# One low part queued earlier and seven w_sp units summed later in an fp32 FNet + gMLP kernel

## The chip, the cores and the metric

The kernel runs on one core of one Trainium2 chip. Its time is the device time of one execution in microseconds (us). Before the change it took 959.19 us, the median of three runs (955.42, 959.19 and 959.47). A core has five engines that each work through a queue of their own: TensorE (PE in the profile, with its weight loads as PEld), VectorE (DVE), ScalarE (ACT), GpSimd (POOL) and SyncE (SP). In this kernel SP issues nearly all loads, and POOL issues nearly all stores.

## The reference

The computation has two residual sublayers over x, 2048 x 512. The six vectors of the modulation come from `silu(c) @ w_mod`.

```python
h = _layernorm(x) * (1 + ca) + sa
x = x + ga * (Cr @ (h @ Hr.T) - Ci @ (h @ Hi.T))        # FNet: 2048x2048 and 512x512 DFT matrices
h = _layernorm(x) * (1 + cb) + sb
z = gelu(h @ w_in)                                      # 2048 x 1792
z1, z2 = z[:, :896], layernorm(z[:, 896:])
g = w_sp @ z2 + b_sp[:, None]                           # w_sp is 2048 x 2048
x = x + gb * ((z1 * g) @ w_out)
```

Everything is fp32.

## The kernel before

**Products.** Each fp32 operand of a product is split into a high part, which ACT makes by a copy that rounds (`ah`, `bh`, ...), and a low part, which DVE makes by subtracting the high part from the operand (`al`, `bl`, ...). `matmul3` (lines 93 to 97) adds three matmuls: high by high, then two with a low part on one side. For z2 the third of the three is the one that reads `al`.

**Chunks.** The left sides of the products come in chunks of 128 x 512, counted by n over the whole kernel. `prep(n)` (line 179) prepares ahead of their use: the high part of chunk n+3 (`prep_hi`, with the transpose or addition on DVE that forms the chunk) and the low part of chunk n+2 (`prep_lo`). `prep_lo` keeps a set of the chunks done, so that a second call for the same chunk does nothing. The order of instructions on each engine is the order in which this program text issues them (the schedule is written out by hand), and each engine works through its queue in that order. `at(n, f, ...)` puts a call on a list for chunk n, and `run(n)` issues what is listed.

**Stages.** The chunks below N2 = 128 are the DFT matrices (tiles `gp`, `yp`). From N2 to N3 = 144 is z1: four groups of four chunks of h2 are reloaded (`stage<-h_d`), transposed (L188, `tt`) and multiplied by the first half of w_in; GELU of the sums goes to DRAM (`z_d`, L618). The first group is loaded a second time for z2. From N3 to N4 = 172 is z2: seven products (order 1, 6, 7, 4, 5, 3, 2; a Strassen-like scheme over 2 x 2 blocks) of four chunks each. z2 is worked in pairs of chunks: `mm_z2(n)` for even n - N3 issues 24 matmuls over chunks n and n+1, six for each of four PSUM banks, the first three of a six with chunk n and the last three with chunk n+1. So there are 14 pairs; products 1, 6, 7, 4, 5, 3 and 2 have pairs 1-2, 3-4, 5-6, 7-8, 9-10, 11-12 and 13-14. Then comes W, the product with w_sp (tiles `gw`), and the output.

**Emptying PSUM.** `empty_z(p, gg)` (line 635) follows the matmuls of a pair. For products 1, 6 and 7 ACT copies the four banks out, for 2 and 4 it applies GELU. For products 5 and 3 DVE adds each bank to what is kept (L649, the additions out of PSUM), and ACT applies GELU to the sum (L652); for product 3 ACT also puts another part back into the bank (L651).

**Units of w_sp.** W uses sums of blocks of w_sp. They are made ahead of it in 16 units. `load_s` (line 662) loads a unit: two transfers of 512 KB into a tile `sj`. `sum_s` does it in two halves: first L673 and L674, then L677 and L678, each half two operations on DVE followed by two stores of 256 KB to `s_d` (L681, issued by POOL). The first nine units fall into the DFT stage, the last seven into z1 and z2. For these seven there are four buffers, so that the load of the fifth waits for the stores of the first, and so on. On SP the loads of the units share one queue with the loads of `stage` (h2 in z1; blocks of w_sp at L159 for W).

**What is issued per chunk in z2.** `prep(n)`, then `run(n)` (with the sums of the units, `hi_w` and `lo_w`, which split the weights of the next product, and `form1`), then for even n - N3 the matmuls of the pair and `empty_z`. So the second low part of the next pair, chunk n+3, comes with `prep(n+1)`, behind the additions of `empty_z`.

Of the kernel before, what the change touches and what calls it, by code (L numbers as in the profile page):

```python
# [19 lines left out]
def fnet_gmlp_kernel(  # L20
# [102 lines left out]
    def at(n, f, *a):  # L123
        fill.setdefault(n, []).append((f, a))

    def run(n):
        for f, a in fill.pop(n, []):
            f(*a)
# [10 lines left out]
    N2 = 4 * len(src)  # L139
    src += h2_d + h2_d[:1]  # L140
    N3 = N2 + 4 * NQ
# [37 lines left out]
    def prep(n):  # L179

        if n not in prepared:
            prepared.add(n)
            prep_hi(n + 3)
            prep_lo(n + 2)
# [9 lines left out]
    def slot(i, name, dtype=F32):  # L194
        return slots[0].tile([P, Q], dtype, tag=f"slot{i}", bufs=1, name=name)
# [11 lines left out]
    def prep_hi(n):  # L207
        if n >= NE:
            return
        if N3 <= n < N4:  # L210
            p = ZPROD[(n - N3) // 4]
            gg, kk = divmod((n - N3) % 4, 2)
            if p == 6:
                T[n] = S2[gg, kk] = bpool[0].tile([P, Q], F32, tag=("bh", "bl")[kk], bufs=3, name=f"s2_{gg}{kk}")
                nc.vector.tensor_tensor(T[n], TT[2 + kk, gg], TT[kk, gg], op=ALU.subtract)
            else:
                T[n] = TT[kk + (2 if p in (2, 4, 3) else 0), gg + (2 if p in (1, 2, 5) else 0)]
        else:
            b, k = divmod(n, 4) if n < N3 else (len(src) + (n - N4) // 4, (n - N4) % 4)
            if N2 + 4 <= n < N3:  # L220
                g = (n - N2) // 4
                T[n] = TT[k, g] = slot(4 * g + k - 4, f"tt{g}_{k}")
            else:
                T[n] = blocks.tile([P, Q], F32, tag="t", bufs=2, name=f"t{n}")
            if n >= N4:
                squares(T[n], stage[b][:, k % 2], k // 2)
            elif n < N2:
                squares(T[n], stage[b], k)
            else:
                turn_block(T[n], b, k)  # L230
        AH[n] = blocks.tile([P, Q], F32R, tag="ah", bufs=4, name=f"ah{n}")
        nc.scalar.activation(AH[n], T[n], AF.Copy)  # L232
        if not N2 <= n < N4 and k == 3:
            stage.pop(b)
            load(b + 2)
# [3 lines left out]
    def prep_lo(n):  # L239
        if n >= NE or n in lows:  # L240
            return
        lows.add(n)
        if N3 <= n < N4 and (n - N3) % 4 == 3:
            AL[n] = slot(16, f"al{n}", F32R)
        else:
            AL[n] = blocks.tile([P, Q], F32R, tag="al", bufs=3, name=f"al{n}")
        t = T.pop(n)
        nc.vector.tensor_tensor(AL[n], t, AH[n].bitcast(F32), op=ALU.subtract)  # L248
        if NZ[4] <= n < NZ[4] + 4:
            gg, kk = divmod(n - NZ[4], 2)  # L250
            nc.vector.tensor_tensor(t, TT[2 + kk, 2 + gg], S2.pop((gg, kk)), op=ALU.subtract)
# [368 lines left out]
    def mm_z2(n):  # L620
        p = ZPROD[(n - N3) // 4]
        gg = (n - N3) % 4 // 2
        fresh = p in (1, 5)
        a = [(AH.pop(m), AL.pop(m)) for m in (n, n + 1)]
        for r in range(4):
            q = 4 * gg + r
            ts = slice(r * P, (r + 1) * P)
            if fresh:
                ZT[q] = bank((4 + q) % 8, f"z2p{p}_{q}")
            for kk, (th, tl) in enumerate(a):  # L630
                matmul3(ZT[q][:, :ZP], th[:, ts], tl[:, ts], WJ[p][:, 0, kk, :ZP], WJ[p][:, 1, kk, :ZP],
                        fresh and kk == 0, kk == 1, not fresh)
        empty_z(p, gg)
# [243 lines left out]
    for s, n in ((4, 4), (5, 4), (6, 6), (7, 6), (8, 10), (9, 10)):  # L877
        m = n + (s == 9)
# [23 lines left out]
    for j, turn, weigh, row, fold, hi in ((0, (25, 26, 27, 28), (29, 29, 30, 30), 26, (34, 34, 35, 36), (38, 35, 36, 37)),  # L902
# [8 lines left out]
        n = weigh[3] + (3 if j == 0 else 1)  # L911
# [13 lines left out]
    for t in range(NQ):  # L925
        n = 8 * NQ * (t + 1)
# [49 lines left out]

    at(90, change_q)
    at(N2, change_s)
    when = [90 + 4 * i for i in range(9)] + [N2 + d for d in (6, 9, 12, 15, 18, 22, 26)]
    for n, u in zip(when, ((r, g, b) for g in range(2) for b in range(4) for r in range(2))):  # L980
        at(n, load_s, *u)
        at(n + 3, sum_s, *u, True)
        at(n + 4, sum_s, *u, False)
    for n in range(N2):
        prep(n)
        mm_a(n)
# [30 lines left out]
    for i, p in enumerate(PROD):  # L1017
        for k in range(8):
            n = NB[p] + 2 * k
# [10 lines left out]
    for f in range(NF):  # L1030
        n = N4 + 24 + 8 * f
# [3 lines left out]
        at(n + 6, make_wo_lo, f)  # L1035
    for n in range(N3, N4):
        prep(n)
        run(n)
        if (n - N3) % 2 == 0:
            mm_z2(n)  # L1040
# [96 lines left out]
```

## Time and profile before

| | us |
|---|---|
| median of three runs | 959.19 |
| time of the profiled execution | 956.25 |
| its span, first to last instruction | 954.3 |
| mean granted TensorE clock | 0.998 of full speed |

A row of the profile's list of instructions begins with its start and its length in us; then come engine, line, operation and tiles (written <- read), and in brackets how long the engine had been idle before it and what ended the idle time. A row of a line's answer gives its instructions with the shortest, median and longest duration in ns and the first and last start in us; the row on landing gives the time from the issue of a transfer until its data is there. Matmul rows overlap, so their pace is read from the distance of their starts.

### The profile page before, as it was taken

To read this page: it belongs to the slowest core of one execution; us is meant where nothing else is said; L and a number is where in the kernel's file an instruction comes from. 1 tells how busy PE (TensorE), PEld (TensorE's weight loads), DVE (VectorE), ACT (ScalarE), POOL (GpSimd) and SP (SyncE) were. 2 spreads that over 40 slices of the span, in tenths; PEclk is the share of its full clock that TensorE was granted. 3 is DMA by queue.
4 is the path that set the end of the run, shared out by engine and by line. 5 is a ranking of instruction groups with operands and counts; after the bars stand their busy time and mean duration, and the time that the engine had idled before them with its cause. 6 is when DMAs were issued, how large, how long until landed. Compare 5 with 4: busy or idle time off the path is not lost.

```text
span 954.3 us, 12323 instructions
## 1 busy us (share of the span) xinstructions
PE 942.3 (99%) x4150; PEld 780.5 (82%) x4150; DVE 712.7 (75%) x1156; ACT 392.0 (41%) x680; POOL 168.1 (18%) x330
## 2 busy tenths in 40 slices
PE   9999999999999999999999899999999999999998
PEld 5888888888888888888888798888888888888886
DVE  7799957785566768875546677999799889886662
ACT  4694424332232212322434577765545454331221
POOL 2330000111520345124323310232000000000000
PEclk9999999999999999999999999999999999999999
DMA  9995652766446787994868920443555465744541
GB/s 213 223 223 121 133 139 65 175 171 165 141 111 147 228 248 218 294 319 128 255 224 265 369 116 1 104 118 89 129 132 137 100 149 122 185 103 161 177 176 55
DMA packets 243344, 158.11 MB, mean 166 GB/s; under 512 B 130001, under 2 KB 212177, under 8 KB 243153
## 3 DMA queue, kind: packets, MB, share of 16 engines
q1 hardware_dynamic: 231520, 119.70, 51.5%
q0 software_dynamic: 11424, 37.24, 10.6%
q8 instruction: 32, 0.52, 0.2%
q10 hardware_dynamic: 336, 0.39, 0.1%
q14 instruction: 32, 0.25, 0.1%
HBM read 120.59 MB, written 36.70 MB: 165 GB/s over the span
## 4 chain that ended last, share of the span: by engine, by line
PE 92%; DVE 3%; DMA 2%; SPq 1%; issue 1%; ACT 1%; POOL 0%; DVEq 0%; ACTq 0%; POOLq 0%
PE gp L96 12%; PE gp L97 12%; PE gp L95 12%; PE gw L97 10%; PE gw L96 10%; PE gw L95 9%; PE yp L95 3%; PE yp L97 3%; PE yp L96 3%; PE op L96 3%; PE op L95 3%; PE op L97 3%; PE z2p L97 2%; PE z1p L95 2%; PE z1p L96 2%; PE z1p L97 2%
## 5 line engine op out<-in xcount | busy, mean ns | idle before, releaser
L232 ACT ACTIVATE ah<-t 128x512 fp32r<-128x512 f32 x244 | 154.1, 632 | 373.0 <-DVE t L175 231.5
L248 DVE TENSOR_TENSOR al<-t,ah 128x512 fp32r<-128x512 f32 x244 | 164.9, 676 | 72.1 <-PE gp L96 45.8
L95 PE MATMUL gp<-ah,hh 128*128 128x512 f32 x496 | 192.9, 389 | 0.0
L96 PE MATMUL gp<-al,hh 128*128 128x512 f32 x496 | 192.9, 389 | 0.0
L97 PE MATMUL gp<-ah,hl 128*128 128x512 f32 x496 | 192.9, 389 | 0.0
L175 DVE STREAM_TRANSPOSE t<-stage 128x512 f32<-128x512 f32 x240 | 168.7, 703 | 7.1 <-DMA stage<-in_A_dft_seq_re_dram 2.7
L97 PE MATMUL gw<-ah,bl 128*128 128x512 f32 x400 | 155.7, 389 | 0.0
L95 PE MATMUL gw<-ah,bh 128*128 128x512 f32 x400 | 155.6, 389 | 0.0
L96 PE MATMUL gw<-al,bh 128*128 128x512 f32 x400 | 155.6, 389 | 0.0
L95 PEld LDWEIGHTS gp<-ah,hh 128*128 128x128 f32 x496 | 93.1, 188 | 19.4
L96 PEld LDWEIGHTS gp<-al,hh 128*128 128x128 f32 x496 | 93.1, 188 | 19.3
L97 PEld LDWEIGHTS gp<-ah,hl 128*128 128x128 f32 x496 | 93.1, 188 | 19.3
L96 PEld LDWEIGHTS gw<-al,bh 128*128 128x128 f32 x400 | 75.1, 188 | 15.7
L97 PEld LDWEIGHTS gw<-ah,bl 128*128 128x128 f32 x400 | 75.1, 188 | 15.7 <-DVE bl L709 0.3
L95 PEld LDWEIGHTS gw<-ah,bh 128*128 128x128 f32 x400 | 75.1, 188 | 15.6
L681 POOL DMA_DIRECT2D s_d<-sj x64 | 34.8, 545 | 129.1 <-DVE sj L673 95.9
L248 DVE TENSOR_TENSOR al<-tt,ah 128x512 fp32r<-128x512 f32 x36 | 24.4, 679 | 34.3 <-PE z1p L96 25.7
L95 PE MATMUL yp<-hth,gh 128*128 128x512 f32 x128 | 49.8, 389 | 0.0
L96 PE MATMUL yp<-htl,gh 128*128 128x512 f32 x128 | 49.8, 389 | 0.0
L97 PE MATMUL yp<-hth,gl 128*128 128x512 f32 x128 | 49.8, 389 | 0.0
L97 PE MATMUL z2p<-wj,al 128*128 128x448 f32 x112 | 42.3, 378 | 6.1 <-DVE al L248 6.1
L95 PE MATMUL z1p<-ah,wih 128*128 128x512 f32 x112 | 43.6, 389 | 0.0
(171 smaller groups left out, 1408.6 us busy)
## 6 DMA issues: line engine op xcount, KB each, us to landing
stage<-in_A_dft_seq_im_dram SPq DMA_DIRECT2D x64, 256.0 KB, 5.3
sj<-in_B_w_sp_dram SPq DMA_DIRECT2D x32, 512.0 KB, 7.9
s_d<-sj POOLq DMA_DIRECT2D x64, 256.0 KB, 5.4
stage<-s_d SPq DMA_DIRECT2D x128, 128.0 KB, 2.8
stage<-in_A_dft_seq_re_dram SPq DMA_DIRECT2D x60, 256.0 KB, 4.8
stage<-in_B_w_sp_dram SPq DMA_DIRECT2D x96, 128.0 KB, 3.3
z_d<-z POOLq DMA_DIRECT2D x28, 256.0 KB, 6.6
stage<-h_d SPq DMA_DIRECT2D x20, 256.0 KB, 5.9
```

The lines of the kernel that those rows point to most:

```text
L95: nc.tensor.matmul(acc, ah, bh, start=first, stop=False, skip_group_check=go_on)
L96: nc.tensor.matmul(acc, ah, bl, start=False, stop=False, skip_group_check=go_on)
L97: nc.tensor.matmul(acc, al, bh, start=False, stop=last, skip_group_check=go_on)
L175: nc.vector.transpose(dst.rearrange("p (b i) -> p b i", i=32), block[:, :, 32 * k:32 * k + 32])
L232: nc.scalar.activation(AH[n], T[n], AF.Copy)
L248: nc.vector.tensor_tensor(AL[n], t, AH[n].bitcast(F32), op=ALU.subtract)
L681: nc.gpsimd.dma_start(s_d[m, r, g][b * P:(b + 1) * P, :], a)
```

## The change

Two places are edited. In the list of units, each of the seven units of z1 and z2 gets a new place: loads at N2 + 4, 7, 10, 13, 17, 21, 25 in place of N2 + 6, 9, 12, 15, 18, 22, 26, and the first half of the sum six chunks behind the load in place of three (the second half one chunk later, as before). So the loads come one or two chunks earlier and the sums one or two chunks later. The nine units before them stay. In the loop over z2, `prep_lo(n + 3)` is called for every even n - N3, behind `prep(n)` and ahead of `run(n)` and `mm_z2(n)`; the call in `prep(n+1)` then does nothing.

```diff
     at(N2, change_s)
-    when = [90 + 4 * i for i in range(9)] + [N2 + d for d in (6, 9, 12, 15, 18, 22, 26)]
-    for n, u in zip(when, ((r, g, b) for g in range(2) for b in range(4) for r in range(2))):
+    when = [(90 + 4 * i, 3) for i in range(9)] + [(N2 + d, 6) for d in (4, 7, 10, 13, 17, 21, 25)]
+    for (n, m), u in zip(when, ((r, g, b) for g in range(2) for b in range(4) for r in range(2))):
         at(n, load_s, *u)
-        at(n + 3, sum_s, *u, True)
-        at(n + 4, sum_s, *u, False)
+        at(n + m, sum_s, *u, True)
+        at(n + m + 1, sum_s, *u, False)
...
     for n in range(N3, N4):
         prep(n)
+        if (n - N3) % 2 == 0:
+            prep_lo(n + 3)
         run(n)
         if (n - N3) % 2 == 0:
             mm_z2(n)
```

No instruction is added or removed. On PE and ACT the order of instructions is the same. On DVE the sums of the units and the low parts move. On SP the loads of the second, third and fourth of the seven units each stand one place ahead of a `stage` load that they stood behind; on POOL the first two stores of the third unit stand behind the seven `z_d` stores that they stood ahead of.

## The prediction

> **What bounds the kernel now.** I read the page first, for the engine that sets the end and for how much of the span it idles; then TensorE's own waits and the times of its matmuls around them; then the engine that it waits for, back to the transfer behind it. All times are us.
>
> ```profile
> span 954.3 us, 12323 instructions
> PE 942.3 (99%) x4150; PEld 780.5 (82%) x4150; DVE 712.7 (75%) x1156; ACT 392.0 (41%) x680; POOL 168.1 (18%) x330
> PE 92%; DVE 3%; DMA 2%; SPq 1%; issue 1%; ACT 1%; POOL 0%; DVEq 0%; ACTq 0%; POOLq 0%
> ```
>
> TensorE (PE) is busy for 942.3 of 954.3 and carries 92% of the chain that ended last. The change takes no matmul away, so it can only gain in the 12 in which PE stands, or where its matmuls run slowly. Among PE's waits one name matters: z2's third term behind `al`, 6 waits, 6.1. The matmul rows place them. z2 consists of 14 pairs of chunks, 24 matmuls each; it starts one pair ahead of 529.01, at about 524.15, and ends at 601.79, where the first `gw` row stands.
>
> ```profile
> 529.01 0.36 PE L95 MATMUL z2p<-wj,ah 128*128 128x448 f32 x1
> 533.88 0.36 PE L95 MATMUL z2p<-wj,ah 128*128 128x448 f32 x1
> ...
> 534.69 0.36 PE L96 MATMUL z2p<-wj,ah 128*128 128x448 f32 x1
> 539.46 0.47 PE L97 MATMUL z2p<-wj,al 128*128 128x448 f32 x1 [4.40 <-DVE al L248]
> ...
> 544.96 0.36 PE L95 MATMUL z2p<-wj,ah 128*128 128x448 f32 x1
> ```
>
> Pair 2 runs from 529.01 to 533.88: 4.87, an undisturbed pair. Pair 3 runs from 533.88 to 544.96: 11.08, so 6.21 too long. Of these, 534.69 to 539.46 is 4.77 for a step of 0.20: 4.57 of standing. The other 1.64 comes after the wait:
>
> ```profile
> 539.46:543.60 4.14, 4.14 (x13) 3.71 (x14) 4.11 (x7) 2.24 (x5) 1.08 (x2) 0.59 1.04 401
> 575.00:602.00 27.00, 25.35 (x118) 21.50 (x117) 21.12 (x37) 22.23 (x41) 3.36 (x9) 1.00 0.00 1
> ```
>
> Columns: length, busy time of PE, weight loads, DVE, ACT and POOL, granted clock, DMA share, GB/s. In the 4.14 behind the wait the clock is 0.59, and the DMA engines are full (1.04). The Trainium skill has a rule for it ("TensorE: Matmul & The Clock Gate", Part 1: The HAM clock gate): about 3.4 us idle halves the clock, and about 3.4 us of work restores it. This trace agrees (4.57 idle, about 4 slow), and by that rule a wait cut to under 3.4 would lose the slow stretch too.
>
> The last five pairs are the second place:
>
> ```profile
> 574.15 0.36 PE L95 MATMUL z2p<-wj,ah 128*128 128x448 f32 x1
> ...
> 575.62 0.47 PE L97 MATMUL z2p<-wj,al 128*128 128x448 f32 x1 [0.30 <-DVE al L248]
> ...
> 592.14 0.47 PE L97 MATMUL z2p<-wj,al 128*128 128x448 f32 x1 [0.46 <-DVE al L248]
> ...
> 597.84 0.47 PE L97 MATMUL z2p<-wj,al 128*128 128x448 f32 x1 [0.31 <-DVE al L248]
> 601.79 0.39 PE L95 MATMUL gw<-ah,bh 128*128 128x512 f32 x1
> ```
>
> Pairs 10 to 14 take 601.79 - 574.15 = 27.64 where 5 x 4.87 = 24.35 would do: 3.3 too long, each time at the sixth matmul of a pair, the first that reads the pair's second low part. Together z2 is 9.5 longer than its matmuls. That is all there is to win.
>
> **Why pair 3 stands.** Its second low part is behind the fourth unit's sum (u4; u1 to u7 are the seven w_sp units of z1 and z2) on DVE:
>
> ```profile
> 530.31 0.69 DVE L248 TENSOR_TENSOR al<-s,ah 128x512 fp32r<-128x512 f32 x1 [1.50 <-ACT ah L232]
> 536.78 0.69 DVE L673 TENSOR_TENSOR sj<-sj 128x512 f32<-128x512 f32 x1 [5.77 <-DMA s_d<-sj]
> ...
> 538.72 0.68 DVE L248 TENSOR_TENSOR al<-s,ah 128x512 fp32r<-128x512 f32 x1
> ```
>
> DVE does pair 3's first low part at 530.31, waits 5.77 in L673, does two sums and an L215, and comes to the second low part at 538.72. The row names a store (`s_d<-sj`) as what came last. I checked that against the landings, since the change moves loads:
>
> ```profile
> L668 SPq DMA_DIRECT2D sj<-in_B_w_sp_dram x2: 910/914/918, 524.5 to 525.5; - x2
> DMA to landing us min/median/max: 7.9/9.5/11.2
> ...
> L681 POOL DMA_DIRECT2D s_d<-sj x2: 539/540/542, 523.4 to 524.2; - x2
> DMA to landing us min/median/max: 4.2/4.3/4.4
> ...
> L681 POOL DMA_DIRECT2D s_d<-sj x2: 539/539/539, 529.1 to 529.8; - x2
> DMA to landing us min/median/max: 10.0/10.3/10.5
> ```
>
> The stores land at 528 to 529 and at 539 to 540, neither at 536.8. The second half of u4's own load, issued at 525.5, lands 11.2 later, at 536.7: that is what L673 waited for.
>
> ```profile
> 483.70 2.31 SPq L153 DMA_DIRECT2D stage<-h_d  x4
> 486.13 3.14 SPq L668 DMA_DIRECT2D sj<-in_B_w_sp_dram  x2
> ...
> 514.55 1.74 SPq L668 DMA_DIRECT2D sj<-in_B_w_sp_dram  x2
> 516.66 7.71 SPq L159 DMA_DIRECT2D stage<-in_B_w_sp_dram  x8
> 524.54 17.09 SPq L668 DMA_DIRECT2D sj<-in_B_w_sp_dram  x8
> ```
>
> SP issues in order: h2 reload (483.70), u2, a block load, u3 (514.55), a block load (516.66), then u4 to u7 without a break.
>
> **The change part by part.** (1) Units. No instruction is added. On SP each of u2 to u4 moves one place ahead of a `stage` load: u2 now stands before the h2 reload, u3 takes u2's place (486), u4 u3's (514.55), u5 u4's (524.54). The block loads wait for DVE to free `stage`, and what frees it keeps its place on DVE, so I let those slots stand. u4 then lands as u3 did, by about 522 (L673 of u3 waited until 522.46), and its sum, now a chunk later, is due at about 532: covered by 10. u5 in the slot of 524.5 lands at 536.7 with the rows above; its sum stands behind the low parts of pair 5, whose high parts ACT makes only when pair 3 is emptied, 538.75 plus two conversions: due at about 541.8, 5 to spare. If that cover fails, the next low part behind it is wanted at pair 6 (533.88 + 3 x 4.87 = 548.5), so the landing may slip to about 546 before PE stands. u6 and u7 wait for the stores of u2 and u3, whose sums come one chunk (2.4) later; due 551 and 562 against landings near 542 and 550. POOL's queue changes in one place: u3's first two stores stand behind seven z1 stores (8 issues of 0.54); only u7's load waits for them. Removed: 4.57 + 1.64 = 6.2. Bounds: 6.2 and, if u5 inherits the wait whole, 0.
>
> (2) Second low parts. In pairs 9 to 12 (products 5 and 3) DVE empties the banks with four additions (L649) that wait for the pair's own matmuls, and the next pair's second low part was behind them:
>
> ```profile
> 574.35 0.62 DVE L649 TENSOR_TENSOR z<-z2p,z 128x448 f32<-128x448 f32 x1 [0.59 <-PE z2p L97]
> 574.89 0.68 DVE L248 TENSOR_TENSOR al<-tt,ah 128x512 fp32r<-128x512 f32 x1
> ```
>
> The last addition waits for the last bank, at 574.15, so the low part ends at 575.5; the sixth matmul was due at 575.2. In the new order it needs only its high part, which ACT makes 1 to 3 into the pair (588.0 at the latest below, in the pair that precedes 592.14's): 0.6 later it is ready, about 2 ahead of the sixth matmul of the next pair. Pair 14's share of the 3.3 is the distance of the sixth matmuls, 597.84 - 592.14 = 5.70, less 4.87: 0.8. Pairs 10 to 13 hold the other 2.5, and that goes.
>
> What is late next is ACT:
>
> ```profile
> 582.90 0.55 ACT L651 ACTIVATE z2p<-z 128x448 f32<-128x448 f32 x1
> ...
> 586.88 1.14 ACT L232 ACTIVATE ah<-tt 128x512 fp32r<-128x512 f32 x2
> ...
> 595.25 1.14 ACT L232 ACTIVATE ah<-tt 128x512 fp32r<-128x512 f32 x2
> ```
> ```profile
> 595.90 0.69 DVE L248 TENSOR_TENSOR al<-tt,ah 128x512 fp32r<-128x512 f32 x1 [2.51 <-ACT ah L232]
> 597.13 0.65 DVE L248 TENSOR_TENSOR al<-tt,ah 128x512 fp32r<-128x512 f32 x1
> 600.83 0.68 DVE L709 TENSOR_TENSOR bl<-z,bh 128x512 fp32r<-128x512 f32 x1
> ```
>
> For product 3 ACT needs 582.90 to 586.88, 4.0, to empty a pair, then 1.1 for two high parts, and about 1 for a weight or a scaling: 6.1 against a pair of 4.87. For two pairs it falls behind by 2.5, which the high parts' lead of about 2 to 2.5 takes up. Following each engine's order, I get pair 14's high part at about 0.1 after the pair's start and its second low part about 0.3 late, so pair 14 keeps about half a microsecond. And the first `bl` of stage W, 0.8 ahead of its use before (600.83 + 0.6 against the third `gw` matmul, 602.26), now stands behind one more low part (0.6) and starts from this later ACT: another 0.5. Against pair 14's old 0.8 that is 0.2 more. Bounds for pairs 10 to 14 with that start: all 3.3 won, or all 3.3 given back.
>
> The sum: -6.2 - 2.5 + 0.2 = -8.5 on the profiled run's own time, 956.25 (its span 954.3 and 1.95 around it): 947.75. The three runs had 955.42, 959.19 and 959.47, so the median lies 2.9 above that run. If those 2.9 are a longer landing wait, they go too; if they lie elsewhere, they stay (950.7). I take 949.0.
>
> **Rivals.** *ACT limits the end of z2 anyway*: the low parts are early but the high parts are not, and the 3.3 comes back in pairs 12 to 14 and the start of W. For it: the 2.51 that DVE waited for `ah` at 595.90, and 22.23 of 27.00 busy on ACT. Against: at pairs 10 to 12 the wait follows an addition, not ACT. Gain 6.2: 950.1 on the run's own time, some 951.5.
>
> *The landing wait moves to u5*: the same place in the queue (524.54), the same full DMA engines. Against: 5 of cover, 9 before PE stands, and one megabyte of load is gone from the burst, moved to about 470. If it took half the wait below the slow-clock point, 2.3 of 8.5 would be lost: 951.5; the whole, 955.
>
> *Slower: the h2 reload is held behind u2's load.* SP cannot pass an instruction that waits. u2's load now stands before the reload, whose first reader is:
>
> ```profile
> 502.54 1.30 DVE L188 STREAM_TRANSPOSE tt<-stage 128x512 f32<-128x512 f32 x2
> ```
>
> If the space of u2 came free only in mid-z1, the reload would go out that much after 483.70; with some 6 to land it may go at 496 at the latest. It decides past that: to eat the 8.5 it must be held to about 505, and at 512 the kernel is at 963. Against: u2 waits for nothing but work of stage Y, and in the trace u1, of the same space, went out 15 ahead of the reload. The Trainium skill says that ScalarE's and VectorE's queues are strict FIFO ("TensorE: Matmul & The Clock Gate", Architectural detail). The 5.77 in L673 with a ready low part behind it agrees, and the new order meets the same rule where a low part now waits for ACT ahead of the additions; that is the first rival.
>
> *Nothing to see*: the runs' own scatter of 4 hides it.
>
> **How the numbers follow.** Forecast 0.73; ACT 0.12; u5 0.08; slower 0.04; nothing 0.03. A change of under 0.5% (4.8) cannot be told from none here; 0.5% below 959.19 is 954.4. Faster: the forecast, ACT and about half of u5's cases, less some for scatter: 0.85; same 0.11; slower 0.04. The range takes the full 9.5 with the lower offset (945.5 to 946) and half of u5's case with the upper (954).
>
> **What would show it.** Right: z2 lasts 68.5 to 69.5 instead of 77.6; no stretch of low clock after the start; L673 without a DMA wait; pairs 3 and 10 to 13 at 4.87; a few tenths at pair 14 or at the first `gw` matmuls, with `ah` or `bl` named. Wrong in part (1): a wait of L673 on a transfer in u5 to u7, with PE waiting behind it. Wrong in part (2): waits for `al` in pairs 12 to 14 of over 2 in sum, with ACT without a gap. Wrong altogether: PE waits in z1, or anywhere after 620, that are not there now.

## The result, and the profile after

| us | before | after |
|---|---|---|
| median | 957.83 (5 runs, 955.13 to 959.47) | 948.92 (5 runs, 948.71 to 950.48) |
| time of the profiled execution | 956.25 | 948.71 |
| its span | 954.3 | 946.8 |

The ratio of the medians is 0.9917, with a 95% interval of 0.9893 to 0.9941: the changed kernel is about 0.8% faster. The first thing to read is the page again: the span, the busy time of the engines and the chain that ended last, by engine.

```profile
span 946.8 us, 12325 instructions
PE 938.3 (99%) x4150; PEld 778.9 (82%) x4150; DVE 712.3 (75%) x1156; ACT 391.7 (41%) x680; POOL 168.2 (18%) x330
...
PE 97%; DVE 1%; ACT 1%; DMA 1%; POOL 0%; issue 0%; SPq 0%; DVEq 0%
```

The five engines' counts of instructions are those of the page before; the total is two higher (12325 against 12323), and the page does not show which two these are. The work of DVE, ACT and POOL is the same to within 0.4. PE's busy time fell by 4.0 with the same 4150 matmuls, in part because none in z2 runs at the low clock any more, and in part because it is 1.6 lower in the first 60, where z2's start loses only 0.24. Its share of the chain rose from 92% to 97%: what was removed was waiting. What is left of it is in PE's waits (the engine and line, what it waited for, then us in all, times, and the longest):

```profile
PE gp L432 <- ACT ah L232: 1.8, 1, 1.8
PE busyp L337 <- DVE busy L276: 1.5, 1, 1.5
PE z2p L95 <- ACT ah L232: 0.6, 1, 0.6
PE gw L97 <- DVE bl L709: 0.3, 1, 0.3
PE gp L432 <- ACT hh L408: 0.3, 1, 0.3
```

The 6.1 of z2's third term behind `al` are gone. In their place stand 0.6 behind a high part (`ah`) and 0.3 at the start of W. The matmul rows place both; these are the starts of pairs 1, 3, 4, 10, 13 and 14, then the third matmul of pair 14 (the first that reads a low part), and the first and third `gw`:

```profile
524.39 0.36 PE L95 MATMUL z2p<-wj,ah 128*128 128x448 f32 x1
...
534.12 0.36 PE L95 MATMUL z2p<-wj,ah 128*128 128x448 f32 x1
538.99 0.36 PE L95 MATMUL z2p<-wj,ah 128*128 128x448 f32 x1
...
568.17 0.37 PE L95 MATMUL z2p<-wj,ah 128*128 128x448 f32 x1
582.76 0.36 PE L95 MATMUL z2p<-wj,ah 128*128 128x448 f32 x1
588.35 0.47 PE L95 MATMUL z2p<-wj,ah 128*128 128x448 f32 x1 [0.57 <-ACT ah L232]
589.08 0.47 PE L97 MATMUL z2p<-wj,al 128*128 128x448 f32 x1
593.66 0.39 PE L95 MATMUL gw<-ah,bh 128*128 128x512 f32 x1
594.60 0.50 PE L97 MATMUL gw<-ah,bl 128*128 128x512 f32 x1 [0.31 <-DVE bl L709]
```

Pair 3 takes 538.99 - 534.12 = 4.87, an undisturbed pair, and so do pairs 10 to 12, 582.76 - 568.17 = 14.59 for three. Pair 13 takes 5.59, because pair 14's first matmul stands behind its high part, and pair 14 takes 5.31, the 0.44 too much in its first matmuls: together 1.18 too long. z2 lasts 593.66 - 524.39 = 69.27 in place of 77.6, 8.4 less. From this W's first matmuls give back 0.6 (the first six `gw` starts span 1.74 in place of 1.15), and z2 starts 0.24 later than before; the rest of the span agrees with the old one, 7.5 less in all.

The window that held the slow clock before (same columns as there) has these numbers now:

```profile
539.46:543.60 4.14, 4.14 (x22) 3.84 (x21) 4.07 (x7) 2.84 (x6) 0.52 (x1) 1.00 1.04 391
```

22 matmuls fit into the 4.14 where 13 did, at a clock of 1.00. The DMA engines are as full as before (1.04), but PE no longer waits for a transfer in that stretch. How close this is, the rows of SP's queue, of the fifth unit's load (u5) and of DVE show:

```profile
513.71 1.50 SPq L668 DMA_DIRECT2D sj<-in_B_w_sp_dram  x2
516.91 10.70 SPq L159 DMA_DIRECT2D stage<-in_B_w_sp_dram  x8
527.78 11.54 SPq L668 DMA_DIRECT2D sj<-in_B_w_sp_dram  x6
```
```profile
L668 SPq DMA_DIRECT2D sj<-in_B_w_sp_dram x2: 615/1331/2047, 527.8 to 528.4; - x2
DMA to landing us min/median/max: 8.8/10.1/11.4
```
```profile
532.66 0.68 DVE L673 TENSOR_TENSOR sj<-sj 128x512 f32<-128x512 f32 x1
542.10 0.69 DVE L673 TENSOR_TENSOR sj<-sj 128x512 f32<-128x512 f32 x1
```

u4 now goes out with 513.71, and its sum at 532.66 has no bracket, so no wait. u5 takes the place behind the block load of L159. That block load needs 10.70 to go out (7.71 before), so u5 leaves at 527.78 and not at 524.5. Its second half lands at 528.4 + 11.4 = 539.8, and the sum at 542.10 finds it there: 2.3 to spare.

The last reading is of ACT at the end of z2, where the new wait comes from:

```profile
580.73 1.14 ACT L232 ACTIVATE ah<-tt 128x512 fp32r<-128x512 f32 x2
...
582.90 1.14 ACT L119 ACTIVATE z<-z,nmrz,rsz 128x896 f32<-128x896 f32 x1 [1.04 <-POOL nmrz L115]
583.95 0.53 ACT L651 ACTIVATE z2p<-z 128x448 f32<-128x448 f32 x1
...
587.69 1.14 ACT L232 ACTIVATE ah<-tt 128x512 fp32r<-128x512 f32 x2
```

ACT stands 1.04 for a factor of the layer norm from POOL (`nmrz`), scales a chunk, empties pair 12 from 583.95 on, and converts pair 14's two high parts only from 587.69. Pair 14 could have started at 582.76 + 4.87 = 587.63.

### The profile page after: what moved, and what is told of

The parts are those of the page before. It is cut to its first block, busy times and chain, and to the rows that moved or that the text cites. A ratio compares the mean times of both kernels' runs of the same rounds, so it can differ in the third digit from the quotient of the medians.

```text
span 946.8 us, 12325 instructions
## 1 busy us (share of the span) xinstructions
PE 938.3 (99%) x4150; PEld 778.9 (82%) x4150; DVE 712.3 (75%) x1156; ACT 391.7 (41%) x680; POOL 168.2 (18%) x330
## 4 chain that ended last, share of the span: by engine, by line
PE 97%; DVE 1%; ACT 1%; DMA 1%; POOL 0%; issue 0%; SPq 0%; DVEq 0%
PE gp L96 12%; PE gp L97 12%; PE gp L95 12%; PE gw L97 10%; PE gw L96 10%; PE gw L95 10%; PE yp L95 3%; PE yp L97 3%; PE yp L96 3%; PE op L96 3%; PE op L95 3%; PE z1p L97 3%; PE z1p L95 3%; PE op L97 3%; PE z1p L96 3%; PE z2p L97 2%
## 5 line engine op out<-in xcount | busy, mean ns | idle before, releaser
L232 ACT ACTIVATE ah<-t 128x512 fp32r<-128x512 f32 x244 | 154.0, 632 | 373.6 <-DVE t L175 234.7
L248 DVE TENSOR_TENSOR al<-t,ah 128x512 fp32r<-128x512 f32 x244 | 164.8, 676 | 70.9 <-PE gp L96 45.5
L248 DVE TENSOR_TENSOR al<-tt,ah 128x512 fp32r<-128x512 f32 x36 | 23.9, 683 | 38.6 <-PE z1p L96 28.6
L96 PE MATMUL z1p<-al,wih 128*128 128x512 f32 x112 | 43.6, 389 | 0.0
```

Source lines behind the costliest of these rows:

```text
L96: nc.tensor.matmul(acc, ah, bl, start=False, stop=False, skip_group_check=go_on)
```

## The experiments

Each edit is made to the changed kernel. The theory was: the units' new places remove pair 3's wait, by taking the fourth unit's load out from behind the block load; the low parts' new place removes the waits of pairs 10 to 13; what is left at the end of z2 is ACT's. The rivals are named with the runs. The first four ran beside the kernel before at a median of 958.75 (955.1 to 960.85), the last four beside it at 957.3 (952.41 to 958.69).

**The low parts alone (e1).** The units go back to their old places.

```diff
-    when = [(90 + 4 * i, 3) for i in range(9)] + [(N2 + d, 6) for d in (4, 7, 10, 13, 17, 21, 25)]
+    when = [(90 + 4 * i, 3) for i in range(9)] + [(N2 + d, 3) for d in (6, 9, 12, 15, 18, 22, 26)]
```

> Only the second low part is queued early; the units are where they were. My account: the fourth unit's load still goes out behind the block load and lands at about 536 to 537, so L673 still waits about 5. Pair 3 no longer pays, since both its low parts are ahead of the sum; but the addition that forms a chunk of pair 4 (L215) stands behind the sum, so PE stands at pair 4 for about 2.5 in all, under the length at which the clock fell, and no slow stretch follows. The last pairs are as in the changed kernel. That makes the changed kernel's 948.9 plus 2.5: 951.4. Rival, only the low parts behind the sum matter: no wait of PE at all and 949. Rival, the landing wait stays whole: pair 3 or 4 too long by 6.2 with a slow stretch, 955.

Measured: 951.5 (950.09 to 954.59), ratio 0.9933 (0.9914 to 0.9953). DVE's rows around the fourth unit's sum (u4), and PE's row behind it:

```profile
537.00 0.69 DVE L673 TENSOR_TENSOR sj<-sj 128x512 f32<-128x512 f32 x1 [4.38 <-DMA sj<-in_B_w_sp_dram]
540.27 0.68 DVE L215 TENSOR_TENSOR s<-tt,tt 128x512 f32<-128x512 f32 x1
540.87 0.68 DVE L248 TENSOR_TENSOR al<-s,ah 128x512 fp32r<-128x512 f32 x1
...
541.61 0.47 PE L97 MATMUL z2p<-wj,al 128*128 128x448 f32 x1 [1.12 <-DVE al L248]
```

The landing wait is back (4.38 on DVE), now with the load itself as its name. But a low part queued early stands ahead of the sum, so PE loses 2.4 in pairs 3 and 4 and not 6.2, and in this execution its clock stays up. In two of the other five it was 0.996 and 0.998 over the span, and they took 954.59 and 954.13; no profile shows what happened in them. So the second edit by itself takes most of the sting out of the first wait, which the prediction did not say. Something else appears that no account holds: pairs 5 to 12 take 4.96 each and not 4.87, at a clock of 1.00. These are the rows of one line of z2's matmuls (shortest, median and longest duration in ns), first here and then in the changed kernel:

```profile
L95 PE MATMUL z2p<-wj,ah x112: 362/368/477, 524.7 to 596.2; 128*128 128x448 f32 x112
```
```profile
L95 PE MATMUL z2p<-wj,ah x112: 362/365/468, 524.4 to 593.0; 128*128 128x448 f32 x112
```

That is some 0.8 over the eight pairs. With the 2.4 it makes up the profiled execution's 951.88 against 948.71. The cause of the slower pace stays open.

**The units alone (e2).** The two added lines are removed.

```diff
-        if (n - N3) % 2 == 0:
-            prep_lo(n + 3)
```

> Only the units are moved; the second low part comes behind the additions as before. My account: L673 waits for no transfer, pairs 1 to 9 take 4.87 each, pairs 10 to 14 are 3.3 too long in sum, and the first gw matmuls wait for nothing. Against the changed kernel that is plus 3.3, less the 1.2 that its pairs 13 and 14 and the 0.6 that its first gw matmuls lose: 950.4. Rival, pair 3 was freed by its low part standing ahead of the sum and not by the load: the wait at pair 3 is back, 955.

Measured: 950.45 (950.14 to 950.84), ratio 0.9917 (0.9902 to 0.9931). Pairs 1 to 9 take 4.87, no L673 waits for a transfer, and the waits at the sixth matmuls of the late pairs are where they were before:

```profile
570.17 0.47 PE L97 MATMUL z2p<-wj,al 128*128 128x448 f32 x1 [0.30 <-DVE al L248]
...
586.64 0.47 PE L97 MATMUL z2p<-wj,al 128*128 128x448 f32 x1 [0.46 <-DVE al L248]
```

Pairs 10 to 14 take 5.43, 5.44, 5.43, 5.66 and 5.62: 3.2 too long, and W starts without a wait. So each edit does what it was forecast to do where it was forecast. From the medians, the units are worth 6.9 to 8.3 (957.3 and 958.75, the two medians of the kernel before that stand above, less 950.45), and the low parts on top of them 950.45 - 948.97 (the changed kernel, run again below) = 1.5. The rows of the two profiles agree: z2 is 71.36 - 69.27 = 2.1 shorter with the low parts, and W's start takes 0.6 of it back.

**The loads early, the sums at their old chunks (e3).**

```diff
-    when = [(90 + 4 * i, 3) for i in range(9)] + [(N2 + d, 6) for d in (4, 7, 10, 13, 17, 21, 25)]
+    when = [(90 + 4 * i, 3) for i in range(9)] + [(N2 + d, m) for d, m in ((4, 5), (7, 5), (10, 5), (13, 5), (17, 4), (21, 4), (25, 4))]
```

> The second low part early and the loads at their new places, but the sums at their old chunks, five or four behind the load. My account: the place of the load on SP is enough: the fourth unit has landed by 522 and waits for nothing; the fifth, landing at 537 to 540 and wanted at about 538, may hold DVE for up to 2 with PE covered. 949 within 0.7. Rival, the six chunks between load and sum are the cover: DVE waits reach PE in pairs 4 to 6, 951 to 955.

Measured: 949.56 (948.65 to 950.07), ratio 0.9905 (0.9888 to 0.9921). u4 has no wait. u5 is waited for: the second half of its load left at 531.0 and landed 10.2 later, at 541.2. The row gives a store as its name, and one did land at about the same time, but the sum reads only the loaded tile:

```profile
541.35 0.69 DVE L673 TENSOR_TENSOR sj<-sj 128x512 f32<-128x512 f32 x1 [3.16 <-DMA s_d<-sj]
...
545.03 0.47 PE L97 MATMUL z2p<-wj,al 128*128 128x448 f32 x1
```

DVE loses 3.16 and PE about 0.5, in pair 5. In the changed kernel the later sum, at 542.10, is what covers u5.

**The sums late, the loads at their old places (e4).**

```diff
-    when = [(90 + 4 * i, 3) for i in range(9)] + [(N2 + d, 6) for d in (4, 7, 10, 13, 17, 21, 25)]
+    when = [(90 + 4 * i, 3) for i in range(9)] + [(N2 + d, m) for d, m in ((6, 4), (9, 4), (12, 4), (15, 4), (18, 5), (22, 5), (26, 5))]
```

> The second low part early and the sums at their new, later chunks, but the loads at their old places on SP. My account: the fourth unit lands at about 536.7 again and L673 waits 4 to 5, but what pair 4 needs first is now ahead of the sum, so PE stands for 0.3 at most: 949.3. Rival, the place of the load is the whole of the cover: pair 4 stands over 2, 951.5 or more.

Measured: 951.82 (950.23 to 954.18), ratio 0.9935 (0.9915 to 0.9954). The median missed my account's number and met the rival's. The profiled execution (950.57) lies between the two: pair 4 lost 1.73, where the account allowed 0.3 and the rival asked for over 2. Either way the place of the load is most of u4's cover, and a later sum does not replace it.

```profile
532.21 0.69 DVE L215 TENSOR_TENSOR s<-tt,tt 128x512 f32<-128x512 f32 x1
538.24 0.69 DVE L673 TENSOR_TENSOR sj<-sj 128x512 f32<-128x512 f32 x1 [5.35 <-DMA sj<-in_B_w_sp_dram]
540.18 0.68 DVE L248 TENSOR_TENSOR al<-s,ah 128x512 fp32r<-128x512 f32 x1
...
540.91 0.47 PE L97 MATMUL z2p<-wj,al 128*128 128x448 f32 x1 [1.21 <-DVE al L248]
```

The two halves of u4's load left at 527.9 and 529.2, behind the long block load, and landed 8.8 to 8.9 later, the second at 538.1. DVE stood 5.35 in L673. The addition that forms a chunk (L215) was done ahead of it, but that chunk's low part (L248) stood behind it, and PE waited for that.

**The changed kernel again, and W's first chunk without the early low part (e5).**

> The changed kernel once more, beside the three that follow. 948.9 within 0.8; a mean granted clock of 1.00 in most executions, where the kernel before had 0.994 to 0.998 in all of its.

Measured: 948.97 (948.64 to 949.16), ratio 0.9922 (0.9903 to 0.9942). The clock was 0.999 or 1.0 in all six executions. The kernel before missed its part of the expectation: two of its 11 executions beside them had 1.0 too.

```diff
-        if (n - N3) % 2 == 0:
+        if (n - N3) % 2 == 0 and n + 3 < N4:
             prep_lo(n + 3)
```

> The changed kernel, but the low part of the second chunk of stage W is no longer queued ahead; the other thirteen are. My account: the first bl goes one low part earlier on DVE, and the 0.6 that the first gw matmuls lose is gone; pairs 13 and 14 keep their 1.2. 948.3. Rival, the first gw matmuls wait because ACT comes late to bh: the 0.6 stays, 948.9.

Measured: 948.25 (948.07 to 948.44), ratio 0.9915 (0.9894 to 0.9936), 0.7 below the changed kernel beside it. DVE's `bl` and PE's third `gw` matmul:

```profile
593.51 0.68 DVE L709 TENSOR_TENSOR bl<-z,bh 128x512 fp32r<-128x512 f32 x1
...
594.36 0.40 PE L97 MATMUL gw<-ah,bl 128*128 128x512 f32 x1
```

W starts at 593.89 and its third matmul comes 0.47 later, without a bracket; in the changed kernel it comes 0.94 later. The call for the chunk behind z2's end was what delayed W, and nothing in z2 needed it: pairs 13 and 14 stay at 5.58 and 5.29.

**Pairs 13 and 14: the layer norm's calls earlier (e6).** W's first product needs z2 normalized, and these calls fall into the end of z2. Beside the edit above:

```diff
-                at(n - 7, norm_z, k)
-                at(n - 6, scale_z, k)
+                at(n - (9 if k < 4 else 7), norm_z, k)
+                at(n - (8 if k < 4 else 6), scale_z, k)
```

> As e5, and the layer norm of the first four z2 tiles two chunks earlier, so that ACT no longer waits for GpSimd's result between the high parts and the emptying of pair 12. My account: ACT's work per pair is the bound there, not that wait alone, since the scaling only moves one pair ahead; 0.3 to 0.5 of the 1.2 goes: 947.9. Rival, the wait for GpSimd (1.0) is what makes pair 14 late: all of its first wait (0.7) goes, 947.5.

Measured: 948.67 (948.37 to 948.87), ratio 0.992 (0.99 to 0.9939). Both expectations missed.

```profile
577.38 1.14 ACT L119 ACTIVATE z<-z,nmrz,rsz 128x896 f32<-128x896 f32 x1 [0.80 <-POOL nmrz L115]
...
583.21 1.12 ACT L119 ACTIVATE z<-z,nmrz,rsz 128x896 f32<-128x896 f32 x1
584.67 0.55 ACT L651 ACTIVATE z2p<-z 128x448 f32<-128x448 f32 x1 [0.35 <-DVE z L649]
...
588.43 1.13 ACT L232 ACTIVATE ah<-tt 128x512 fp32r<-128x512 f32 x2
```

The wait for POOL moved to 577.38, one pair earlier, and the scaling at 583.21 stands directly ahead of the emptying as before. The high parts came at 588.43, 0.7 later than in the changed kernel, and pairs 13 and 14 took 6.18 and 5.38. So the edit did not take the wait away: it put a wait of 0.80 and one more scaling (1.14) ahead of pair 11's emptying, and all that follows on ACT came later. What the wait for POOL by itself costs is not shown by this run.

**Pair 14's high parts ahead of pair 12's emptying (e7).** Beside the edit of W's first chunk, the two high parts get two buffers that are free there, and are issued one pair earlier:

```diff
     def prep_hi(n):
-        if n >= NE:
+        if n >= NE or n in highs:
             return
+        highs.add(n)
...
-        AH[n] = blocks.tile([P, Q], F32R, tag="ah", bufs=4, name=f"ah{n}")
+        if n - N4 in (-2, -1):
+            AH[n] = slot(6 + n - N4, f"ah{n}", F32R)
+        else:
+            AH[n] = blocks.tile([P, Q], F32R, tag="ah", bufs=4, name=f"ah{n}")
...
+        if n == N4 - 6:
+            prep_hi(n + 4)
+            prep_hi(n + 5)
```

> As e5, and the two high parts of pair 14 are made ahead of the emptying of pair 12 (they get two free buffers of their own). My account: pair 14 waits because its high parts stand behind eight operations of ACT; ahead of them they fall into ACT's wait of 1.0 for GpSimd and cost nothing. Pairs 13 and 14 take 4.87 each and z2 takes 68.1: 1.2 less than e5, 947.1. Rival, ACT is full there whatever the order: what pair 14 gains, the high parts of stage W lose, and the time is that of e5.

Measured: 946.87 (946.7 to 947.16), ratio 0.9901 (0.988 to 0.9922), below both kernels: 2.1 under the changed kernel beside it and 1.4 under e5, as my account had it. ACT, DVE and PE (lines from L232 on are numbered six higher here):

```profile
580.53 2.18 ACT L238 ACTIVATE ah<-tt 128x512 fp32r<-128x512 f32 x4
582.71 1.14 ACT L119 ACTIVATE z<-z,nmrz,rsz 128x896 f32<-128x896 f32 x1
...
585.82 1.24 DVE L254 TENSOR_TENSOR al<-tt,ah 128x512 fp32r<-128x512 f32 x2
...
587.44 0.36 PE L95 MATMUL z2p<-wj,ah 128*128 128x448 f32 x1
592.30 0.40 PE L95 MATMUL gw<-ah,bh 128*128 128x512 f32 x1
```

Four high parts come in one row, at 580.53, ahead of the scaling; it also takes the place in which ACT stood for POOL. Both low parts are done by 587.1, ahead of pair 14's start, and pair 14 takes 592.30 - 587.44 = 4.86, pair 13 the same. At 4.87 a pair z2 has nothing left to win.

## Why the prediction was right

949.0 was forecast and 948.92 measured; the gain came from the two places named, by the mechanisms named. That it landed within 0.1 is luck, because two errors of about 1.0 cancel: the sum on the profiled execution was 947.75 against 948.71, and the step from there to the median was 1.25 against 0.2.

- **Pair 3, -6.2:** right in the profile (4.87, clock 1.00). That the wait was for the load and not for the store in the row's label is borne out by e1 and e4 (the low parts alone, the sums late), where rows for the same sum name the load.
- **u5's cover, 5:** it held, but with 2.3 to spare. The step that failed is "I let those slots stand": the block load ahead of u5 took 10.70 to go out in place of 7.71, so u5 left 3.2 later than assumed. With the sum one chunk earlier (e3) the rival's wait is there, 3.16 on DVE, but for PE it costs only 0.5.
- **Pairs 10 to 13, -2.5:** the waits for `al` went as forecast, and the units alone (e2) have them all. But pair 13 is not 4.87: its last stretch belongs to the next point.
- **Pair 14, about half a microsecond:** the term that was mis-sized. The mechanism was right (ACT's high parts are late next), the size was 1.18 for pairs 13 and 14. The working gave ACT 6.1 per pair for two pairs and no wait of its own; the row at 582.90 shows 1.04 more behind POOL. The profile before had that wait already, 2.45 long:

```profile
590.47 1.14 ACT L119 ACTIVATE z<-z,nmrz,rsz 128x896 f32<-128x896 f32 x1 [2.45 <-POOL nmrz L115]
```

The run with the high parts ahead (e7) removes all 1.18, so ACT's late high parts are its cause. How much of it the wait for POOL makes is not shown: e7 removes that wait too, and e6 only moves it. By an estimate from the rows, without the 1.04 the high parts would start at 587.69 - 1.04 = 586.65, about 1 ahead of where pair 14 could have started.
- **W's start, 0.5 lost:** 0.6 by the rows, and 0.7 came back in the median when the one call was left out (e5).
- **Start-up:** z2 begins 0.24 later. From 20 to 524 PE is busy throughout in both profiles, so this is lost in the first 20, ahead of anything that the change touches. Over all ten profiles z2 begins between 524.15 and 524.92. The first wait for `ah` at L432 (1.8 here, none in the profile before) is not the whole of it: it is 1.0 in the repeated run, where z2 begins at 524.66. With 0.24, 0.7 for pairs 13 and 14, and 0.1 for W, the missing 1.0 of the sum is accounted for.
- **The median's offset:** "if those 2.9 are a longer landing wait, they go too". Nearly all of it went. Over both sets of runs, 20 of the 22 executions of the kernel before had a clock of 0.994 to 0.998 and took 955.1 to 960.85; the two at 1.000 took 952.41 and 952.91. Nine of 11 executions of the changed kernel had 0.999 or 1.0 and took 948.64 to 949.16, two had 0.997 and took 950.48 and 950.23. In e2, e3, e5, e6 and e7, with u4's load at its new place, every execution had 0.999 or more; with it at its old place (e1, e4) they had 0.996 to 1.0. So most of the scatter goes with the place of that load, but not all: the two at 0.997 had it at its new place. The profiled execution of before, at 0.998, was one of the milder ones: the units were worth 6.9 to 8.3 in the medians where its rows gave 6.2. How the slow stretch looked in the other executions no profile shows.

The rivals: ACT at the end of z2 took 1.2 and not 3.3; u5 inherited no wait of PE's; the h2 reload went out behind u2's load at no cost, as no wait of PE in z1 was added; and the runs told the gain from none (the interval of the ratio ends at 0.9941).

The rule of the Trainium skill on idle time and the clock ("TensorE: Matmul & The Clock Gate", Part 1: The HAM clock gate) separates the cases seen: 4.57 of idle was followed by a clock of 0.59, while the waits of 1.12 and 1.21 in the profiled executions of e1 and e4 left it at 1.00 and 0.999 over their spans. No profile has a wait in z2 between 1.21 and 4.57, so the point itself is not measured.

## What to carry to other kernels

A wait on the engine that sets the end is best traced to the landing behind it and not to the name in the brackets, and a transfer behind an instruction that stalls its queue is late by that stall: move it ahead of the stall, rather than its reader further back (e4 against e3). When a group of waits is removed, work out the next engine's order with its own waits in it, and issue what the bound engine needs next ahead of the bulk work: in e7 two high parts moved ahead of an emptying won 1.4 over e5. Compare a profiled execution's clock with that of the others before its rows are summed: in the kernel before it differed from 0.994 to 1.000, and the times differed with it.

## What was not expected of the hardware

- Issuing is not of constant length: the same eight block loads took 7.71 on SP's queue before and 10.70 after, with the DMA engines full in both (1.11 and 1.05 from 516.9 to 527.6), and what stood behind them left that much later. It took 8.04 in e2, the other kernel without the early low parts, and 9.48 to 11.71 in the eight profiles with them. So the length seems to go with the second edit and not with the units' places; why is not shown.
- PE's pace in z2 was not quite fixed at a clock of 1.00: a pair took 4.96 in e1's pairs 5 to 12, and 4.87 elsewhere, as a distance of starts of 0.207 against 0.203 per matmul. No wait goes with it, and it is there where the DMA engines stand nearly idle. In the same stretch, e1 has 49 matmuls (first row) and the changed kernel 51 (second row):

```profile
571.29:581.21 9.92, 9.92 (x49) 9.01 (x48) 8.03 (x13) 7.04 (x14) 0.00 (x0) 1.00 0.01 2
571.29:581.21 9.92, 9.92 (x51) 9.19 (x50) 8.44 (x15) 8.30 (x16) 0.08 (x1) 1.00 0.00 0
```

- One mean of the clock over the span, 0.994 to 1.000, sorted the executions of the kernel before roughly by their time, where all looked like plain scatter of 0.9%.
